# mLSTM cell and hash-routed experts: first step's gate rows moved on the chip, second chunk's gates as a group of their own

## The chip, the cores and the metric

The kernel runs on one core of one Trainium2 chip. The metric is device time in microseconds for one execution; the median of three runs stands for the kernel. Engines are named as the profile names them: PE (TensorE), DVE (VectorE), ACT (ScalarE), POOL (GpSimd), SP (SyncE, which mostly issues DMAs).

## The reference, cut to what matters

Two blocks follow each other. The first is an mLSTM cell over 4 batches, 8 heads, 768 time steps and head dimension 40; the second sends each of the 3072 rows of 320 numbers to one of 8 experts, chosen by a hash of its token id.

```python
for t in range(S):
    m_new = np.maximum(f_gate[:, :, t] + m, i_gate[:, :, t])
    f_stab = np.exp(f_gate[:, :, t] + m - m_new)
    i_stab = np.exp(i_gate[:, :, t] - m_new)
    m = m_new
    C = f_stab[:, :, None, None] * C + i_stab[:, :, None, None] * np.einsum('bhd,bhe->bhde', vt, kt)
    n = f_stab[:, :, None] * n + i_stab[:, :, None] * kt
    h_tilde = np.einsum('bhde,bhe->bhd', C, qt)
    y[:, :, t] = o * h_tilde / denom
...
expert_idx = token_ids * np.int64(2654435761) % np.int64(E)
h = np.maximum(xe @ w1[e], 0.0)
out[mask] = h @ w2[e]
```

## The kernel before, in words

The recurrence is worked out in chunks of 128 time steps. There are 6 chunks and 4 batches, so 24 steps `s`, with batch `b = s % 4` and chunk `c = s // 4`; the loop over them is `for s in range(NT)`. Steps 0 to 3 are the first chunk and need no earlier state. All instructions stand in program order for each engine's queue (`manual_schedule`), so the order written in the code is the order in which an engine takes its work, and an instruction that waits holds up all behind it on that engine. That holds for SP's DMAs too.

A step needs k, q and v of its 128 time steps (`load`, 160 KB each, six buffers of each), and its gates. Inside a chunk, the weight between two time steps is the exponential of a sum of gate terms. The kernel makes that sum by a product of two small bf16 operands: `L`, whose rows 0 to 23 hold the terms of the column's time step (the "ends" e, each split into 3 bf16 pieces, for 8 heads), and `R`, whose rows 32 to 37 hold the terms of the row's time step (A, and from the second chunk on X, 3 pieces each). The other rows of `R` and `L` are constants (selectors, a mask). There are two `L` tiles, one a chunk in turn, and four `R` tiles, one a step in turn.

The class `Gates` computes these terms on DVE for a group of batch-heads and chunks: `sums` gives A, `ends` gives e, `split` makes the 3 pieces (two subtractions), `rows` copies the bf16 halves into the tile `zt` (on ACT), and `weights` makes the factors for k (an exponential on ACT, a transpose on PE, a copy on DVE into `kwT`). There are three groups: `g0` for chunk 0 on 32 partitions, `g1` for chunks 1 to 4 on 128 partitions, `g2` for chunk 5 on 32 partitions, which reuses g0's tiles. `g1` takes its running maxima from `m_d` in DRAM, to which the scan of all 768 time steps (`m_sb`) is written. `keep` writes `zt` to DRAM, `load_a(s)` brings a step's rows back into `R` and `load_e(c)` a chunk's ends into `L`; both are issued by SP. The constant part of `R` is made once in `Rs[0]` and copied on DVE to `Rs[1]`, `Rs[2]`, `Rs[3]`.

A step consists of: `turn` (PE transposes k and q, ACT copies them out of PSUM), `scores` (PE products of k and q, 16 matmuls), `decays` (PE products of `L` and `R` at L333, exponentials on ACT at L337; later chunks also scale q, at L345), `weigh` (DVE multiplies scores by decays, L375), `k_weights` (POOL scales k, L355), `state` (PE, new state, L400), `attend` (PE, L421 and L427) and `divided` (DVE, L436 to L440). In pass `s` of the loop PE takes, in order, `turn(s + 2)`, `scores(s + 1)`, `decays(s + 1)`, `state(s)`, `attend(s)`. The scores' PSUM tiles have one buffer each, so `scores(s + 1)` waits for `weigh(s)`. The tag `tr` (two buffers) serves the transposes, the tag `xh` (two buffers) the results of a step; `divided(s - 1)` frees the buffer that `state(s)` opens.

Before the loop, `unread` makes products that nobody reads (9, 8 and 3 of them). Inside the loop, SP issues in each pass: `load_a(s + 3)`, k and q of step `s + 5`, v of step `s + 4`, then gate loads `o` (listed in `o_at`), and later stores of finished rows. `sigmoid` runs over 8 steps' gates at once at the end of passes 7, 12 and 17. The routing of the experts is cut into pieces that are placed in certain passes (`pieces`, `products`): the transposed ids in pass 4 and a scan of counts in pass 5, for instance. The expert layers come after the loop and are not touched.

## Time and profile before

| | us |
|---|---|
| median of 3 runs | 390.69 |
| lowest and highest run | 388.94, 391.33 |
| profiled execution, its own time | 388.61 |
| its span (first to last instruction) | 386.7 |
| busy in the span: PE, DVE, ACT, POOL | 366.6, 138.0, 113.0, 143.8 |
| mean granted PE clock | 0.987 |

The first stage, the 24 steps, takes about the first 137 us of the span; the expert layers take the rest. In a timeline or chain row the first number is the start in us from the span's start, the second the duration in us, and the arrow in brackets names what ended the engine's idle time before it. `SPq` and `ACTq` rows are DMA issues: the time that the queue's engine took to issue, not the time of the transfer. In the rows of stretches come the stretch and its length, busy us and instruction count of PE, PE's weight loads, DVE, ACT and POOL, then the clock that PE was granted, the mean busy share of the 16 DMA engines, and GB/s.

### The profile page before, as it was taken

To read this page: it belongs to the slowest core of one execution; us is meant where nothing else is said; L and a number is where in the kernel's file an instruction comes from. 1 tells how busy PE (TensorE), PEld (TensorE's weight loads), DVE (VectorE), ACT (ScalarE), POOL (GpSimd) and SP (SyncE) were. 2 spreads that over 40 slices of the span, in tenths; PEclk is the share of its full clock that TensorE was granted. 3 is DMA by queue.
4 is the path that set the end of the run, shared out by engine and by line. 5 is a ranking of instruction groups with operands and counts; after the bars stand their busy time and mean duration, and the time that the engine had idled before them with its cause. 6 is when DMAs were issued, how large, how long until landed. Compare 5 with 4: busy or idle time off the path is not lost.

```text
span 386.7 us, 7979 instructions
## 1 busy us (share of the span) xinstructions
PE 366.6 (95%) x3211; PEld 255.7 (66%) x3211; DVE 138.0 (36%) x355; ACT 113.0 (29%) x232; POOL 143.8 (37%) x247
## 2 busy tenths in 40 slices
PE   7699999899999889999999999999999999999991
PEld 7587788788888666865665655565565665664560
DVE  8657887787878921212012012002102102101100
ACT  5376467576495301111011011111111111101100
POOL 8442555898987317231142140124024020020120
PEclk9789999999999999999999999999999999999998
DMA  6698899989998689382731721442262000000000
GB/s 136 118 175 159 149 171 177 197 191 194 182 232 241 190 272 348 128 251 90 233 108 51 245 97 33 153 160 65 94 215 68 0 34 17 0 35 16 2 26 25
DMA packets 124220, 51.02 MB, mean 132 GB/s; under 512 B 104338, under 2 KB 120174, under 8 KB 124182
## 3 DMA queue, kind: packets, MB, share of 16 engines
q1 hardware_dynamic: 116614, 36.73, 40.7%
q0 software_dynamic: 2496, 8.20, 6.4%
q10 hardware_dynamic: 5072, 5.57, 4.6%
q8 instruction: 26, 0.43, 0.5%
q14 instruction: 12, 0.10, 0.1%
HBM read 42.10 MB, written 8.71 MB: 131 GB/s over the span
## 4 chain that ended last, share of the span: by engine, by line
PE 77%; DVE 8%; issue 6%; POOL 3%; ACT 2%; SPq 2%; DMA 1%; POOLq 0%; DVEq 0%; ACTq 0%
PE mh L858 24%; PE zp L887 23%; PE mh L851 7%; PE sp L369 5%; PE tr L322 5%; PE xh L427 3%; PE ab L333 2%; PE xh L421 2%; PE xh L400 2%; PE tp L834 1%; DVE w L375 1%; PE zp L928 1%; POOL out_dram L821 1%; SPq L193 1%; SPq L189 1%
## 5 line engine op out<-in xcount | busy, mean ns | idle before, releaser
L887 PE MATMUL zp<-w2t,h 128*128 128x320 f32 x384 | 105.5, 433 | 0.0
L858 PE MATMUL mh<-xT,w1t 128*128 128x416 f32 (+2 forms) x288 | 97.0, 481 | 1.3 <-DVE x L440 1.3
L887 PEld LDWEIGHTS zp<-w2t,h 128*128 128x128 f32 x384 | 72.6, 190 | 31.5 <-issue 2.9
L858 PEld LDWEIGHTS mh<-xT,w1t 128*128 128x128 f32 x288 | 51.3, 190 | 39.8 <-issue 37.8
L821 POOL DMA_INDIRECT out_dram<-zo,s_idx x26 | 25.7, 988 | 88.7 <-ACT zo L820 88.4
L840 DVE COPY xT<-tp 128x384 f32<-128x384 f32 x15 | 8.4, 558 | 128.0 <-PE tp L836 128.0
L867 ACT ACTIVATE h<-mh 128x416 f32<-128x416 f32 (+2 forms) x36 | 17.2, 479 | 110.0 <-PE mh L851 59.4
L820 ACT COPY zo<-zp 128x320 f32<-128x320 f32 x26 | 11.1, 426 | 101.3 <-PE zp L887 93.1
L865 DVE TENSOR_SCALAR h<-mh 128x416 f32<-128x416 f32 (+2 forms) x36 | 19.6, 543 | 59.2 <-PE mh L851 31.5
L375 DVE TENSOR_TENSOR w<-sp,w 128x512 f32<-128x512 f32 x48 | 30.8, 682 | 10.7 <-ACT w L337 10.7
L427 PE MATMUL xh<-v,w 128*64 128x41 f32 x768 | 34.6, 222 | 0.0
L337 ACT ACTIVATE w<-ab 128x512 f32<-128x512 f32 x48 | 26.0, 594 | 18.9 <-PE ab L333 18.9
L369 PE MATMUL sp<-qT,kT 64*128 64x128 f32 x384 | 29.5, 291 | 1.7 <-DVE w L375 0.9
L959 POOL COPY hrem<-h 128x256 f32<-128x256 f32 x8 | 3.2, 398 | 74.4 <-ACT h L867 74.4
L427 PEld LDWEIGHTS xh<-v,w 128*64 128x64 f32 x768 | 30.5, 138 | 0.0
L109 POOL DMA_INDIRECT xg<-x_rows,g_idx x24 | 23.4, 973 | 15.6 <-PE mh L851 6.8
L369 PEld LDWEIGHTS sp<-qT,kT 64*128 64x128 f32 x384 | 24.7, 193 | 6.0 <-issue 2.8
L851 PE MATMUL mh<-xT,w1c 64*128 64x416 f32 (+2 forms) x144 | 27.9, 497 | 0.1
L421 PE MATMUL xh<-C,qs 128*64 128x82 f32 x320 | 27.3, 249 | 0.0
L410 POOL TENSOR_TENSOR C<-C,add 64x164 f32<-64x164 f32 x32 | 17.7, 552 | 16.4 <-ACT add L404 15.2
L444 POOL TENSOR_TENSOR x<-x,og 128x320 f32<-128x320 f32 x24 | 20.5, 871 | 6.7 <-DVE x L440 4.9
L355 POOL TENSOR_TENSOR kw<-k,kwT 128x320 f32<-128x320 f32 x20 | 14.4, 723 | 13.1 <-DMA q<-in_q_dram 7.7
(188 smaller groups left out, 388.3 us busy)
## 6 DMA issues: line engine op xcount, KB each, us to landing
w2t<-in_moe_w_dram SPq DMA_DIRECT2D x5, 1280.0 KB
w1t<-in_moe_w_dram SPq DMA_DIRECT2D x5, 1024.0 KB
k<-in_k_dram SPq DMA_DIRECT2D x24, 160.0 KB
v<-in_v_dram SPq DMA_DIRECT2D x24, 160.0 KB
og<-in_o_gate_dram SPq DMA_DIRECT2D x24, 160.0 KB
x_rows<-x SPq DMA_DIRECT2D x24, 160.0 KB
q<-in_q_dram SPq DMA_DIRECT2D x23, 160.0 KB
w2t<-in_moe_w_dram ACTq DMA_DIRECT2D x2, 1280.0 KB
```

The lines of the kernel that those rows point to most:

```text
L109: nc.gpsimd.indirect_dma_start(out=xg, out_offset=None, in_=x_d[:rows, :], in_offset=bass.IndirectOffsetOnAxis(ap=idx, axis=0),)
L337: nc.scalar.activation(w[:, hf], ab[:], AF.Exp)
L369: nc.tensor.matmul(sp[hf][:, j, :], lhsT=d["kT"][r, j, :], rhs=d["qT"][r, j, :], start=True, stop=True)
L375: nc.vector.tensor_tensor(d["w"][:, hf], d["sp"][hf][:], d["w"][:, hf], op=ALU.mult)
L421: nc.tensor.matmul(xh[t, 2 * j : 2 * j + 2, :], lhsT=d["qs"][:, j, t], rhs=Cs[b][c % 2][:, j].rearrange("p h d -> p (h d)"), start=True, s ...
L427: nc.tensor.matmul(hs[t, 2 * j + hf, :], lhsT=d["w"][:, hf, j, t], rhs=d["v"][:, 2 * j + hf, :], start=(c == 0), stop=True, skip_group_che ...
L444: nc.gpsimd.tensor_tensor(x[:], x[:], og[s // NG][:, s % NG], op=ALU.mult)
L821: ins = nc.gpsimd.indirect_dma_start(out=out[:, :], out_offset=bass.IndirectOffsetOnAxis(ap=idx, axis=0), in_=zo[:], in_offset=None, bound ...
L851: nc.tensor.matmul(hp[i][:, : c1 - c0], lhsT=w1c[r, fp, :], rhs=xT[r, 2, c0:c1], start=first, stop=not first,)
L858: nc.tensor.matmul(hp[i][:, : c1 - c0], lhsT=w1t[:, db, fb * P : (fb + 1) * P], rhs=xT[:, db, c0:c1], start=(first and db == 0), stop=(not ...
L865: nc.vector.tensor_relu(h[:, 2 * fp, c0:c1], hp[i][:, : c1 - c0])
L887: nc.tensor.matmul(zp[:], lhsT=h[:, fb, j * P : (j + 1) * P], rhs=w[2][:, fb, :], start=(fb == 0), stop=(fb == FB - 1),)
```

## The change

Chunk 0's rows for step 0 (batch 0) are moved from `zt` straight into `Rs[0]` by six small DMAs (`direct_a`, four on SP and two on ACT), and the ends into `Ls[0]` by one DMA a batch (`direct_e`). A rows for steps 1 to 3 still go through DRAM. k and q of step 2 are issued before the remaining small transfers, v of step 0 after k. The writes of pieces are divided into rows (`keep_a`) and ends (`keep_e`), and the ends are laid out so that `load_e` is one DMA instead of three.

Chunk 1 becomes a group of its own, `ga`, on 32 partitions, with g0's tiles; it takes its maxima from `m_sb` on the chip. `g1` then covers chunks 2 to 4 on 96 partitions; its loads (f1, i1, m1) move into pass 0, its work into passes 1 to 6. `g2`'s work moves to later passes. The copies to `Rs[2]` and `Rs[3]` move behind `weigh(0)` and into pass 0; `load_a(3)` moves into pass 1, `load_a(8)` and `load_e(2)` into pass 6. `unread` is called with 9 and 4. Four of the eight memsets of `Cs` go, and `Ls[1]` and `Lx` are made in pass 0.

```diff
-    z0 = nc.dram_tensor("gate_pieces0", (9, BH, P), BF16, kind="Internal").ap()
-    z1 = nc.dram_tensor("gate_pieces1", (9, (NB - 2) * BH, P), BF16, kind="Internal").ap()
-    z2 = nc.dram_tensor("gate_pieces2", (9, BH, P), BF16, kind="Internal").ap()
+    firsts = (0, 1, 2, NB - 1, NB)
+    zx = [
+        nc.dram_tensor(f"gate_rows{i}", (6, (firsts[i + 1] - firsts[i]) * BH, P), BF16, kind="Internal").ap()
+        for i in range(4)
+    ]
+    ze = [
+        nc.dram_tensor(f"gate_ends{i}", ((firsts[i + 1] - firsts[i]) * BH, 3 * P), BF16, kind="Internal").ap()
+        for i in range(4)
+    ]
...
+        MID = (NB - 3) * BH
+        f1 = gp.tile([MID, P], F32, name="f1")
+        i1 = gp.tile([MID, P], F32, name="i1")
+        m1 = gp.tile([MID, P + 1], F32, name="m1")
...
-        kwT0 = gp.tile([P, BH], F32, name="kwT0")
-        kwT1 = gp.tile([P, P], F32, name="kwT1")
+        kwT = gp.tile([P, (NB - 1) * BH], F32, name="kwT")
...
         def pieces_of(c):
-            return (z0, 0) if c == 0 else (z2, 0) if c == NB - 1 else (z1, (c - 1) * BH)
+            g = max(i for i in range(4) if firsts[i] <= c)
+            return g, (c - firsts[g]) * BH
...
         def load_a(s):
             b, c = place(s)
             n = 3 if c == 0 else 6
-            z, r = pieces_of(c)
-            src = z[:n, r + b * H : r + (b + 1) * H].rearrange("i h t -> i (h t)")
+            g, r = pieces_of(c)
+            src = zx[g][:n, r + b * H : r + (b + 1) * H].rearrange("i h t -> i (h t)")
             nc.sync.dma_start(
                 Rs[s % 4][32 : 32 + n].rearrange("i two h t -> i two (h t)"), src.unsqueeze(1).to_broadcast([n, 2, H * P]),
             )
 
         def load_e(c):
-            z, r = pieces_of(c)
-            for i in range(3):
-                nc.sync.dma_start(
-                    Ls[c % 2][i * H : (i + 1) * H], z[6 + i, r : r + BH].rearrange("(b h) t -> h b t", h=H),
-                )
-
-        def keep(z, zt, rows, eng):
-            eng.dma_start(z[rows].rearrange("i r t -> r i t"), zt[:, rows])
+            g, r = pieces_of(c)
+            nc.sync.dma_start(
+                Ls[c % 2][: 3 * H], ze[g][r : r + BH].rearrange("(b h) (i t) -> (h i) b t", h=H, i=3),
+            )
+
+        def keep_a(g, zt, n, eng):
+            eng.dma_start(zx[g][:n].rearrange("i r t -> r i t"), zt[:, :n])
+
+        def keep_e(g, zt, eng):
+            eng.dma_start(ze[g], zt[:, 6:9].rearrange("r i t -> r (i t)"))
+
+        def direct_a(zt):
+            for j in range(2):
+                for i in range(3):
+                    eng = nc.scalar if i == 2 else nc.sync
+                    eng.dma_start(Rs[0][32 + i : 33 + i, j], zt[:H, i])
+
+        def direct_e(b, zt):
+            nc.sync.dma_start(Ls[0][: 3 * H, b], zt[b * H : (b + 1) * H, 6:9])
 
...
-        load(0, "v")
-        for t, src in ((f1, flat[0]), (i1, flat[1])):
-            nc.sync.dma_start(t[:], src[:, P : S - P].rearrange("r (c t) -> c r t", t=P))
...
-            ind[:], ident[: 3 * H, : 3 * H].rearrange("p (i h) -> p h i", i=3), axis=AX,
+            ind[:], ident[: 3 * H, : 3 * H].rearrange("p (h i) -> p h i", i=3), axis=AX,
...
-            def weights(self, dst):
+            def weights(self, dst, tag="tr"):
                 nc.scalar.activation(
                     self.a[:], self.t["e"][:, 0], AF.Exp, bias=self.t["A"][:, 0, P - 1 : P],
                 )
-                tp = ps.tile([P, self.n], F32, name="tpg", tag="tr", bufs=2)
+                tp = ps.tile([P, self.n], F32, name="tpg", tag=tag, bufs=2)
                 nc.tensor.transpose(tp[:], self.a[:], ident[: self.n, : self.n])
-                nc.vector.tensor_copy(dst[:], tp[:])
+                nc.vector.tensor_copy(dst, tp[:])
...
         g0 = Gates(BH, f0[:], i0[:], m0, "zt0")
-        g1 = Gates(P, f1[:], i1[:], m1, "zt1")
+        second = slice(P, 2 * P)
+        ga = Gates(BH, f_sb[:, second], i_sb[:, second], m_sb[:, P : 2 * P + 1], "zta", g0)
+        g1 = Gates(MID, f1[:], i1[:], m1, "zt1")
         last = slice(S - P, S)
         g2 = Gates(BH, f_sb[:, last], i_sb[:, last], m_sb[:, S - P :], "zt2", g0)
...
-                t, r0 = (kwT0, b * H) if c == 0 else (kwT1, (c - 1) * BH + b * H)
+                r0 = c * BH + b * H
...
         g0.sums(True)
         g0.split("A")
         g0.rows("A", nc.scalar.copy)
-        keep(z0, g0.zt, slice(0, 3), nc.scalar)
+        direct_a(g0.zt)
         g0.ends()
         g0.split("e")
         g0.rows("e", nc.scalar.copy)
-        keep(z0, g0.zt, slice(6, 9), nc.scalar)
+        direct_e(0, g0.zt)
+        keep_a(0, g0.zt, 3, nc.sync)
+        load(2, "k")
+        load(0, "v")
+        direct_e(1, g0.zt)
+        load(2, "q")
         unread(9)
         turn(0, "k")
         turn(0, "q")
         nc.vector.tensor_tensor_scan(m_sb[:, 1:], f_sb[:], i_sb[:], NEG, op0=ALU.add, op1=ALU.max)
+        g0.weights(kwT[:, :BH], "xh")
+        ga.sums(False)
         nc.vector.tensor_copy(Rs[1][:], Rs[0][:])
-        nc.scalar.dma_start(m_d, m_sb[:])
-        load_a(0)
-        load_e(0)
-        nc.vector.tensor_copy(Rs[2][:], Rs[1][:])
-        nc.sync.dma_start(m1[:], bass.AP(tensor=m_d.tensor, offset=m_d.offset + P, ap=[[P, NB - 2], [S + 1, BH], [1, P + 1]]))
-        load_a(1)
-        nc.vector.tensor_copy(Rs[3][:], Rs[2][:])
-        load(2, "k")
-        load(2, "q")
-        load(1, "v")
-        load_a(2)
-        unread(8)
+        turn(1, "k")
+        unread(4)
         scores(0)
-        turn(1, "k")
         turn(1, "q")
         for t in ks[3:] + qs[3:]:
             nc.gpsimd.memset(t[:, :, D:], 0.0)
-        for t in sum(Cs, []):
+        for t in [c[1] for c in Cs]:
             nc.gpsimd.memset(t[:], 0.0)
-        ends_rows(Ls[1])
-        nc.gpsimd.tensor_copy(Lx[:], one[:, 1].to_broadcast([P, HB]))
-        g0.weights(kwT0)
         k_weights(0)
-        for i in range(3, KV - 1):
-            load(i, "k")
-            load(i, "q")
-            load(i - 1, "v")
-        unread(3)
         decays(0)
+        load_a(1)
+        direct_e(2, g0.zt)
+        direct_e(3, g0.zt)
+        nc.scalar.dma_start(m_d, m_sb[:])
+        ga.split("A")
+        ga.ends()
+        load(1, "v")
         weigh(0)
-        g1.sums(False)
-        g1.split("A")
-        g1.ends()
-        g1.split("e")
+        ga.split("e")
+        nc.vector.tensor_copy(Rs[2][:], Rs[1][:])
+        load(3, "k")
+        load(3, "q")
+        load_a(2)
+        load(2, "v")
+        load(4, "k")
+        load(4, "q")
+        load(3, "v")
         nsig, ndone, waiting = -1, 0, {}
...
-            if s + 3 < NT and s not in (1, 2):
+            if s + 3 < NT and s not in (0, 1, 5):
                 load_a(s + 3)
             if s + KV - 1 < NT:
                 load(s + KV - 1, "k")
                 load(s + KV - 1, "q")
             if s == 1:
+                load_a(3)
                 load_a(4)
                 load_e(1)
+            if s == 6:
+                load_a(8)
+                load_e(2)
             if s + KV - 2 < NT:
                 load(s + KV - 2, "v")
-            if b == 0 and 0 < c < NB - 1:
+            if b == 0 and 1 < c < NB - 1:
                 load_e(c + 1)
-            if s == 2:
-                load_a(5)
+            if s == 0:
+                for t, src in ((f1, flat[0]), (i1, flat[1])):
+                    nc.sync.dma_start(t[:], src[:, 2 * P : S - P].rearrange("r (c t) -> c r t", t=P))
+                nc.sync.dma_start(
+                    m1[:], bass.AP(tensor=m_d.tensor, offset=m_d.offset + 2 * P, ap=[[P, NB - 3], [S + 1, BH], [1, P + 1]]),
+                )
             for i in o_at.get(s, ()):
                 load(i, "o")
             if s == 2:
                 nc.sync.dma_start(tok[:], moe_token_ids.rearrange("(b c p) -> c b p", b=B, c=NB))
             if s == 13:
-                keep(z2, g2.zt, slice(0, 9), nc.sync)
+                keep_a(3, g2.zt, 6, nc.sync)
+                keep_e(3, g2.zt, nc.sync)
+            if s == 5:
+                keep_a(2, g1.zt, 6, nc.sync)
+                keep_e(2, g1.zt, nc.sync)
             for i in waiting.pop(s, []):
                 store(i)
...
-            if s == 4:
+            if s == 7:
                 nc.scalar.activation(g2.t["X"][:, 0], g2.t["A"][:, 0], AF.Exp)
-            if s in (5, 8, 11):
-                g2.rows({5: "A", 8: "X", 11: "e"}[s], nc.scalar.copy)
+            if s in (7, 10, 11):
+                g2.rows({7: "A", 10: "X", 11: "e"}[s], nc.scalar.copy)
+            if s in (3, 4):
+                g1.rows({3: "A", 4: "e"}[s], nc.scalar.copy)
+            if s == 2:
+                nc.scalar.activation(g1.t["X"][:, 0], g1.t["A"][:, 0], AF.Exp)
...
             if s == 0:
-                nc.scalar.activation(g1.t["X"][:, 0], g1.t["A"][:, 0], AF.Exp)
-                g1.rows("A", nc.scalar.copy)
+                nc.scalar.activation(ga.t["X"][:, 0], ga.t["A"][:, 0], AF.Exp)
+                ga.rows("A", nc.scalar.copy)
...
             if s == 0:
-                g1.split("X")
-                g1.rows("e", nc.scalar.copy)
-                g1.rows("X", nc.scalar.copy)
-                keep(z1, g1.zt, slice(0, 9), nc.sync)
+                ga.split("X")
+                ga.rows("e", nc.scalar.copy)
+                ga.rows("X", nc.scalar.copy)
+                keep_a(1, ga.zt, 6, nc.sync)
+                keep_e(1, ga.zt, nc.sync)
+                nc.vector.tensor_copy(Rs[3][:], Rs[2][:])
+                ends_rows(Ls[1])
+                nc.gpsimd.tensor_copy(Lx[:], one[:, 1].to_broadcast([P, HB]))
...
+            if s == 1:
+                g1.sums(False)
             if s == 2:
-                g1.weights(kwT1)
+                ga.weights(kwT[:, BH : 2 * BH])
+                g1.split("A")
+                g1.ends()
             if s == 3:
+                g1.split("e")
+                g1.split("X")
+                g1.rows("X", nc.scalar.copy)
+            if s == 5:
                 g2.sums(False)
-            if s == 4:
+            if s == 6:
+                g1.weights(kwT[:, 2 * BH :])
                 g2.split("A")
-            if s == 6:
+            if s == 9:
                 g2.split("X")
             if s == 10:
                 g2.ends()
```

More of the change, by code (lines that the diff above doesn't have):

```diff
@@ L166 @@
         m_sb = gp.tile([BH, S + 1], F32, name="m_sb")
-        f1 = gp.tile([P, P], F32, name="f1")
-        i1 = gp.tile([P, P], F32, name="i1")
-        m1 = gp.tile([P, P + 1], F32, name="m1")
+        MID = (NB - 3) * BH
+        f1 = gp.tile([MID, P], F32, name="f1")
+        i1 = gp.tile([MID, P], F32, name="i1")
+        m1 = gp.tile([MID, P + 1], F32, name="m1")
         ones = gp.tile([P, P], F32, name="ones")
         tok = gp.tile([NT, P], I64, name="tok")
-        kwT0 = gp.tile([P, BH], F32, name="kwT0")
-        kwT1 = gp.tile([P, P], F32, name="kwT1")
+        kwT = gp.tile([P, (NB - 1) * BH], F32, name="kwT")
         st, og = {}, {}
@@ L353, in k_weights @@
                 d["kw"] = kws[s % 2]
-                t, r0 = (kwT0, b * H) if c == 0 else (kwT1, (c - 1) * BH + b * H)
+                r0 = c * BH + b * H
                 nc.gpsimd.tensor_tensor(
                     d["kw"][:, :, :D], d["k"][:, :, :D],
-                    t[:, r0 : r0 + H].unsqueeze(2).to_broadcast([P, H, D]), op=ALU.mult,
+                    kwT[:, r0 : r0 + H].unsqueeze(2).to_broadcast([P, H, D]), op=ALU.mult,
                 )
```

## The prediction

> **What bounds the kernel now.** I read the page first: PE is busy 95% of the span, so what counts is where PE is held up or slowed. Next the stretches of 5 us at the start, the only place where the granted clock falls (us busy and count per engine, clock, DMA share, GB/s):
>
> ```profile
> 10.00:15.00 5.00, 2.80 (x21) 1.89 (x19) 3.08 (x5) 2.44 (x5) 3.84 (x5) 0.95 0.25 51
> 15.00:20.00 5.00, 4.21 (x26) 3.31 (x28) 3.29 (x11) 1.17 (x2) 0.00 (x0) 0.50 1.14 202
> 20.00:25.00 5.00, 5.00 (x80) 4.12 (x82) 2.71 (x8) 4.16 (x10) 1.77 (x7) 0.87 1.00 181
> 25.00:30.00 5.00, 5.00 (x112) 4.43 (x108) 2.49 (x7) 3.52 (x8) 2.51 (x13) 1.00 0.76 143
> ```
>
> From 10 to 15 us PE has 2.80 us of work and the DMA engines stand three quarters idle; then the clock is at half: 0.05, 0.50 and 0.13 of a full clock lost in three rows of 5 us, so from about 14.5 to 21.3, 6.8 us. Why, the chain of what ended last in order of time tells (start, us, what):
>
> ```profile
> 6.74 1.74 DVE m_sb L685
> 8.48 1.98 DVE R L686
> 10.48 0.99 DVE R L690
> 11.49 0.99 DVE R L693
> 13.06 2.51 DMA k<-in_k_dram
> ```
>
> The loads of step 2 are issued at 13.06, behind gate-row transfers that wait for DVE and for a write to DRAM. The waits agree, SP's first, then PE's (us in total, times, longest):
>
> ```profile
> SPq L203 <- DMA gate_pieces<-zt: 3.2, 2, 2.3
> PE tr L322 <- DMA k<-in_k_dram: 1.7, 1, 1.7
> ```
>
> ACT's timeline dates the steps, the exponentials of decays(0) to decays(4):
>
> ```profile
> 13.79 1.08 ACT L337 ACTIVATE w<-ab 128x512 f32<-128x512 f32 x2 [1.76 <-PE ab L333]
> 20.59 1.09 ACT L337 ACTIVATE w<-ab 128x512 f32<-128x512 f32 x2 [2.00 <-PE ab L333]
> 25.05 1.09 ACT L337 ACTIVATE w<-ab 128x512 f32<-128x512 f32 x2 [0.24 <-PE ab L333]
> 29.10 1.09 ACT L337 ACTIVATE w<-ab 128x512 f32<-128x512 f32 x2 [0.80 <-PE ab L333]
> 33.97 1.08 ACT L337 ACTIVATE w<-ab 128x512 f32<-128x512 f32 x2 [0.85 <-PE ab L333]
> ```
>
> The full pace is 4.05 us (25.05 to 29.10); decays(0) to decays(1) takes 6.80. So some 4 us could be won before decays(3). SP's queue is the other resource, here with what it issues for decays(2), (3) and the second chunk:
>
> ```profile
> 14.83 0.58 SPq L203 DMA_DIRECT2D R<-gate_pieces  x1
> ...
> 20.86 0.46 SPq L203 DMA_DIRECT2D R<-gate_pieces  x1
> ...
> 23.73 0.37 SPq L215 DMA_DIRECT2D gate_pieces<-zt  x1
> ...
> 27.15 0.29 SPq L203 DMA_DIRECT2D R<-gate_pieces  x1
> ```
>
> Between the first two stand seven loads of 160 KB: 6.03 us, 0.86 a load. R of decays(3) is issued at 20.86, 7.8 us before PE uses it at 28.65.
>
> **The change, part by part.** Times are from the span's start, by durations of these rows.
>
> Rows of step 0 on the chip. Two ACT issues of 0.36 follow the A copy (ends 6.21), so the e copy starts at 6.95 instead of 6.84: 0.1, not on PE's path. SP issues four row DMAs, the ends DMA and the write of the A rows (0.29 to 0.46 each in its rows for R and L), then k2 and v0: k2 goes out near 8.4 (before 13.06) and lands near 10.9 by the chain's 2.51. How soon an on-chip transfer lands no row shows; bounded by R's (10.47 to the products at 13.35, 2.9) and by no gain over its 0.3 of issue, it lies between 8 and 10.6 for issues up to 7.7. Cover: PE gets to decays(0) only near 12.6, so either end costs nothing.
>
> PE's order up to decays(0). ACT copies kT0 and qT0 until 8.6 and makes the weights' exponential (0.40) by 9.05; PE then does tpg 0.24, k1's transposes 0.6, four dummy products 0.94, scores 1.16, q1's transposes 0.6, and the ab products of decays(0) start at 12.6. ACT's copy of q1 (0.59) goes first: exponentials at 13.2 against 13.79, 0.6 won. DVE has copied kwT at 9.6, does ga's sums (1.0) and R1's copy (0.98) until 11.7, ga's A split and ends (1.2) until 12.9, and weighs from 13.8 to 15.1: what was added is hidden in DVE's wait, which was 1.85 here.
>
> Step 1. k2 and q2 are in; scores(1) waits for the weighing and ends at 16.2; R1 was issued at 11.75 and is in. decays(1)'s exponentials come at 16.6: 4.0 ahead. Step 2 follows at the old pace, 20.8 against 25.05.
>
> SP from there is what decides. load_a(2) waits for R2's copy on DVE: weighing ends 15.1, ga's e split 0.6, copy 0.98, so 16.7. SP stands until then, and v2, k4, q4, v3, k5, q5, v4 are queued behind it. Then come the new f1, i1 (0.73, 0.54), m1 (0.55), two writes of ga's pieces (0.37 each), k6 and q6, and only then load_a(3). Lower bound, each at its quickest issue (k 0.4, q 0.57, v 0.4, with 0.05 between): 7.3 us, issue at 24.0. Upper bound, 0.86 for each of nine loads and 3.0 for the rest: 10.7 us, 27.4. I take 25.9, about the middle: the DMA engines start empty near 17 (q3 out at 14.3, and 2.51), but are then given loads faster than they move them. Landing: 2.51 (k2's) to 2.84 us later (the chain has a row `53.28 2.84 DMA R<-gate_pieces`), so R3 is in at 28.4 (26.5 to 30.2). PE has been ready since scores(3), at 24.4. The exponentials of decays(3) follow its first product by 0.45 (28.65 to 29.10), so they come at 28.85 instead of 29.10: of the 4.0 us won, 0.25 is left (1.9 down to -1.5). The wait stands in PE's order before state(2) and attend(2), so nothing else fills it.
> DVE has a second wait here: g1's sums of step 1 need f1, i1 and m1, in near 26; behind them divided(1) (1.1) ends at 28.0, which state(2) waits for. It lies beside R3's wait and costs nothing unless R3 comes before 28.
>
> The clock after that wait. PE stands 4.0 us (24.4 to 28.4). In the trace the clock fell at 14.5 with PE at work for 2.80 us of the five before, its longest wait by then 1.0 us. So I expect another half-clock stretch. Ends: 0, and 3.4 us lost (6.8 at half). I take half of it, 1.7, as PE is dense afterwards, where at 15 to 18 it still waited.
> The Trainium skill (TensorE: Matmul & The Clock Gate, Part 1) has the clock fall after at least one idle window of about 3.4 us and rise after one busy window. By it a 4.0 us wait may or may not fill a free-running window, and would cost 0 or 1.7; here the clock fell without any such wait, so I keep the rows' reading.
>
> Later steps. decays(4) finds R4 and L1 in: the second chunk's pieces are written near 24 instead of 23.73. Step 4 loses g2's A split on DVE (0.27 + 0.48), which held up the copy that q6's successor on PE waited for by 0.24: -0.24 (0 to -0.75). Step 5 gets g2's sums (0.71 + 0.28 + 0.41) ahead of the routing scan, where DVE had 0.39 idle: 0 to 1.1, taken 0.4, since state(7) waited for divided(6) there. Step 6 gets g1's weights: one more transpose, 0.33 (0.24 to 0.8: the row's own time, and with the 0.47 that PE waited for it in step 2). Step 7 needs R8 and L2, whose loads now stand behind k11 and q11: SP was through with those near 51.0, so by 2.84 they would land at 53.9 and 54.3, and decays(8) began at 54.06. SP has three L loads less to issue before that (2.35 us from 40.42) and two writes more: 0 (0 to 1.5). Step 8 loses the X copy between sigmoid and exponentials, 0.4 on the chain. Steps 2 and 3 get 1.2 us of g1's splits on DVE in place of g2's sums (1.4) and of DVE's idle time before qs: 0. The copies of A and e (0.51 each on ACT) lie in ACT's waits for transposes, 1.3 to 1.75 a step; if those go, 0.5 each.
> Fewer L loads (one DMA for three, five times) save SP about 0.7 a time, off the path. POOL writes Ls[1] and Lx (2.5 us) in step 0 instead of before kw: it had 7.7 idle there, and without that kw(2) would start up to 2.5 later.
>
> Sum: -0.25 + 1.7 - 0.24 + 0.4 + 0.33 - 0.4 = +1.54. On the profiled execution (388.61, span 386.7 and 1.9 around it) that is 390.15; the median of the runs, 390.69, lies 2.08 above it, so 392.2. About 1% (3.9 us) is what a measurement of this kernel can tell from no change.
>
> **The rivals.**
> The clock holds through the wait for R3: the same sum without 1.7, so 390.5. For: PE runs at 1.00 in every stretch from 25 to 140 us. Against: the fall at 14.5 us.
> R3 comes in time. If SP gets load_a(3) out by 22, f1 to m1 land by 23.5, divided(1) ends at 25.6 and state(2) starts there instead of at 29.10: -3.5, with the later terms' +0.09 on top 387.3. For: SP's rows hold issues of 0.3 to 0.4 us. Against: 6.03 us for seven loads, and here there are nine and five small ones.
> A cold start, on the slower side. Dummy products fall from 20 to 13, and PE waits from 6.4 to 9.1. If the clock halves at about 11.0, 2.1 us of PE work is left before decays(0)'s exponentials (scores 1.05, q1 0.6, half of ab 0.4) and takes twice as long; the weighing ends at 17.2, load_a(2) goes out at 18.8 and R3 is in at 30.5: +2.1 on the sum, 394.3. It decides from where decays(0)'s exponentials start after 15. For: 2.80 us of PE work in five was already enough for a fall. Against: from 9.1 on PE has no gap over 1 us.
> The same page (Part 4: PE-mode transpose) says that transposes do not count as PE-busy in the same way for the gate. That speaks for this rival, as PE's early work is mostly transposes; no row here separates the two.
>
> **How the numbers follow.** The main sum 0.46, clock holds 0.20, R3 in time 0.15, cold start 0.19. Predicted is the main one, 392.2. The range goes down to 387.0 (R3 in time, with a little over half of it inside) and up to 395.2 (the cold start with 0.9 us of the unknown costs), leaving out about 0.2. Faster by over 1% (below 386.8) is the half of R3 in time in which the later terms take their lower ends too (step 4 -0.75, step 5 0): 0.08. Slower by over 1% (above 394.6): 0.4 of the cold start and the upper end of the main case (clock 3.4, step 5 1.1, step 6 0.8, step 7 1.5), 0.20. Within 1%: 0.72.
>
> **What would show it.** Right: exponentials at about 13, 16.6, 20.8, then 28.9; PE idle for some 4 us before line L333 in step 2, released by a DMA of the gate rows; load_a(3) issued after 25; a half-clock stretch near 28 to 32. Wrong: exponentials every 4.05 us from 16.6 on; first exponentials after 15; or a total that moves by over 4 us.

## The result, and the profile after

The changed kernel takes 395.78 us (median of 4 runs, 395.50 to 396.26) against 390.84 (4 runs) for the kernel before: a ratio of 1.0142, 95% interval 1.0111 to 1.0172. It is slower, by 3.6 us more than predicted, and 0.6 us above the range. The profiled execution took 395.50 us with a span of 393.6 (before: 388.61 and 386.7).

In the changed kernel the lines have moved: exponentials L354, products of `L` and `R` L350, transposes L339, row loads L210, on-chip rows L230, on-chip ends L233, `divided` L453 to L457. First ACT's timeline, which dates the steps 0 to 5, with what stands before the first:

```profile
6.23 1.97 ACTq L230 DMA_DIRECT2D R<-zt  x2
8.24 0.51 ACT L312 COPY zt<-e_zt 32x384 bf16<-32x384 bf16 x1 [2.04 <-DMA R<-zt]
...
16.70 0.60 ACT L354 ACTIVATE w<-ab 128x512 f32<-128x512 f32 x1
...
20.21 1.08 ACT L354 ACTIVATE w<-ab 128x512 f32<-128x512 f32 x2 [1.45 <-PE ab L350]
...
24.30 1.11 ACT L354 ACTIVATE w<-ab 128x512 f32<-128x512 f32 x2
...
33.53 1.09 ACT L354 ACTIVATE w<-ab 128x512 f32<-128x512 f32 x2 [0.93 <-PE ab L350]
...
39.27 1.08 ACT L354 ACTIVATE w<-ab 128x512 f32<-128x512 f32 x2 [0.40 <-PE ab L350]
...
45.09 1.08 ACT L354 ACTIVATE w<-ab 128x512 f32<-128x512 f32 x2
```

The first exponentials are 3.5 us later than predicted (16.70 for 13.2), the fourth 4.7 (33.53 for 28.85). PE's timeline has the two waits that go with these:

```profile
10.06 0.31 PE L324 MATMUL tpg<-ident,a_zt 32*128 32x32 f32 x1 [3.30 <-ACT a_zt L320]
...
32.86 1.06 PE L350 MATMUL ab<-R,L 128*64 128x512 bf16 x4 [4.62 <-DMA R<-gate_rows]
```

SP's timeline shows the queue behind the second of them: the on-chip rows, k of step 2, `load_a(2)`, then f1, i1, m1, the second chunk's pieces, and last `load_a(3)`:

```profile
6.23 2.89 SPq L230 DMA_DIRECT2D R<-zt  x4
...
10.49 0.43 SPq L199 DMA_DIRECT2D k<-in_k_dram  x1
...
19.76 0.26 SPq L210 DMA_DIRECT2D R<-gate_rows  x1
...
25.30 0.81 SPq L759 DMA_DIRECT2D f<-in_f_gate_dram  x1
...
26.94 0.69 SPq L760 DMA_DIRECT2D m<-gate_max  x1
27.74 0.39 SPq L221 DMA_DIRECT2D gate_rows<-zt  x1
...
29.94 1.70 SPq L210 DMA_DIRECT2D R<-gate_rows  x2
```

Stretches of 3.4 us, laid so that the changes of the granted clock fall on their borders (columns as before: PE's busy time is the first after the length, the clock the third from the end):

```profile
6.10:9.50 3.40, 0.67 (x6) 0.42 (x4) 2.30 (x4) 1.36 (x4) 2.56 (x15) 1.00 0.02 3
9.50:12.90 3.40, 2.84 (x13) 2.71 (x13) 2.42 (x5) 1.09 (x3) 2.21 (x3) 0.51 0.48 83
12.90:16.30 3.40, 3.40 (x24) 2.68 (x24) 1.82 (x5) 0.08 (x1) 1.56 (x3) 0.50 0.53 93
...
26.60:30.00 3.40, 1.64 (x22) 1.28 (x19) 0.00 (x0) 1.07 (x2) 1.31 (x9) 1.00 0.53 109
30.00:33.40 3.40, 0.54 (x4) 0.21 (x4) 1.91 (x7) 0.31 (x1) 0.00 (x0) 0.50 0.70 131
33.40:36.80 3.40, 3.40 (x54) 3.16 (x51) 1.37 (x3) 2.07 (x5) 0.00 (x0) 0.50 1.00 179
```

So the clock is at half twice, for 6.8 us each: from 9.5, after a window in which PE worked for 0.67 us, and from 30.0, in the middle of the wait for R3. Both the predicted wait and the rival "cold start" have come.

Where the 6.9 us of the two profiled executions lie is read from the starts of the exponentials (columns other than the first two kernels belong to the experiments below):

| step | before | after | a4 | c1 | e2 | b1 | b2 | d2 |
|---|---|---|---|---|---|---|---|---|
| 0 | 13.79 | 16.70 | 15.47 | 15.54 | 13.99 | 13.69 | 13.67 | 14.47 |
| 1 | 20.59 | 20.21 | 18.98 | 19.05 | 17.52 | 17.19 | 17.17 | 17.97 |
| 3 | 29.10 | 33.53 | 28.52 | 27.87 | 26.65 | 26.28 | 25.92 | 26.72 |
| 5 | 38.23 | 45.09 | 40.29 | 40.10 | 36.38 | 35.41 | 35.05 | 35.85 |
| 7 | 49.69 | 55.20 | 51.31 | 51.12 | 47.26 | 47.52 | 47.23 | 48.04 |
| 8 | 54.52 | 60.59 | 58.00 | 56.51 | 54.30 | 52.34 | 52.06 | 52.87 |
| 9 | 61.49 | 67.85 | 65.50 | 63.75 | 63.42 | 61.27 | 59.04 | 59.85 |
| 11 | 69.82 | 76.18 | 73.83 | 72.08 | 71.76 | 72.26 | 67.37 | 68.19 |

Differences of the first two columns: +4.43 us at step 3, +2.43 from step 3 to 5, -1.35 from 5 to 7, +0.56 from 7 to 8, +0.29 from 8 to 9: 6.36, which then stays (6.36 at step 11).

An exponential can also be late by ACT's own doing, so PE's products of `L` and `R`, which it follows, are the better mark for PE. At steps 3, 5, 7, 8 and 9 they start at 28.65, 37.78, 49.24, 54.07 and 58.90 before and at 32.86, 43.17, 54.76, 60.15 and 64.98 after: +4.21 us at step 3, +1.18 from 3 to 5, +0.13 from 5 to 7, +0.56 from 7 to 8, nothing from 8 to 9. The loss lies at step 3.

### The profile page after: what moved, and what is told of

Same layout as the page of the kernel before. It is cut to its first block, busy times and chain, and to the rows that moved or that the text cites. A ratio compares the mean times of both kernels' runs of the same rounds, so it can differ in the third digit from the quotient of the medians.

```text
span 393.6 us, 7972 instructions
## 1 busy us (share of the span) xinstructions
PE 368.3 (94%) x3198; PEld 257.6 (65%) x3198; DVE 142.0 (36%) x367; ACT 114.1 (29%) x237; POOL 143.2 (36%) x243
## 4 chain that ended last, share of the span: by engine, by line
PE 79%; DVE 8%; issue 5%; POOL 3%; ACT 2%; DMA 1%; ACTq 0%; SPq 0%; POOLq 0%; another core or an unknown queue 0%; DVEq 0%
PE mh L904 23%; PE zp L933 23%; PE mh L897 7%; PE sp L386 5%; PE tr L339 5%; PE xh L444 4%; PE ab L350 3%; PE xh L438 2%; PE xh L417 2%; DVE w L392 2%; PE tp L880 1%; PE zp L974 1%; POOL out_dram L867 1%; PE xb L358 1%; DVE qs L362 1%
## 5 line engine op out<-in xcount | busy, mean ns | idle before, releaser
L444 PE MATMUL xh<-v,w 128*64 128x41 f32 x768 | 35.5, 225 | 0.0
L444 PEld LDWEIGHTS xh<-v,w 128*64 128x64 f32 x768 | 31.5, 141 | 0.0
L354 ACT ACTIVATE w<-ab 128x512 f32<-128x512 f32 x48 | 26.1, 595 | 15.3 <-PE ab L350 15.3
L438 PE MATMUL xh<-C,qs 128*64 128x82 f32 x320 | 27.4, 249 | 0.0
```

What stands on the lines that cost most here:

```text
L354: nc.scalar.activation(w[:, hf], ab[:], AF.Exp)
L438: nc.tensor.matmul(xh[t, 2 * j : 2 * j + 2, :], lhsT=d["qs"][:, j, t], rhs=Cs[b][c % 2][:, j].rearrange("p h d -> p (h d)"), start=True, s ...
L444: nc.tensor.matmul(hs[t, 2 * j + hf, :], lhsT=d["w"][:, hf, j, t], rhs=d["v"][:, 2 * j + hf, :], start=(c == 0), stop=True, skip_group_che ...
```

## The experiments

Theories at the start. A: R3's late load holds step 3. B: the cold start delays all of it. C: g1's sums, which wait on DVE for m1, would hold step 3 as long as R3 does. D: the separate group for the second chunk costs in steps 3 to 9. Each ratio is to the kernel before, on the same chip.

### a1: R3 loaded earlier

```diff
         nc.vector.tensor_copy(Rs[2][:], Rs[1][:])
+        nc.vector.tensor_copy(Rs[3][:], Rs[2][:])
...
             if s == 0:
+                load_a(3)
                 for t, src in ((f1, flat[0]), (i1, flat[1])):
...
             if s == 1:
-                load_a(3)
                 load_a(4)
...
-                nc.vector.tensor_copy(Rs[3][:], Rs[2][:])
```

> The changed kernel with one thing undone in SP's order: the copy to Rs[3] stands beside that to Rs[2], and load_a(3) goes out in pass 0 before f1, i1 and m1, as before the change. Theory A (SP's queue: R3 is late because load_a(3) stands behind gate loads, piece writes, k6 and q6): PE's 4.62 us wait for R3 and the half clock behind it go, 5 to 6 us faster than the changed kernel, about 390. Theory C (DVE: g1's sums wait 4.95 us for m1 on DVE, and divided(1) behind them holds state(2)): the wait only moves from the ab products to state(2), which starts near 33 instead of 33.9, at most 1 us faster, about 395. Theory B (the cold start decides everything) expects no more than 1 us either.

396.15 us, ratio 1.0161 [1.0109, 1.0214]: nothing gained. R3 is in, and PE's products for step 3 run at 27.55. But the exponentials start at 32.31, because DVE stands before g1's sums (DVE's timeline of a1), with `divided(1)` behind them, and ACT stands with it before the exponential of `X`, which needs the sums:

```profile
31.00 0.29 DVE L299 TENSOR_TENSOR a_zt<-f,m 96x128 f32<-96x128 f32 x1 [5.92 <-DMA m<-gate_max]
```

A alone falls; C holds.

### a2: a1, and g1's sums one pass later

```diff
-            if s == 1:
-                g1.sums(False)
             if s == 2:
                 ga.weights(kwT[:, BH : 2 * BH])
+                g1.sums(False)
```

(The exponential of `X` moves with it, to pass 3.)

> As the last one, and g1's sums move from pass 1 to the end of pass 2 (its X exponential to pass 3). Theory A with C: both waits that end near 33 are gone, decays(3) at about 28.5 and every step after it 4 to 5 us earlier, no half clock at 30: 5 to 6 us faster than the changed kernel, 390 to 391. If A alone were right it would equal the last run within 0.5. If B alone were right, both stay near 395.

394.08 us, ratio 1.0111 [1.0053, 1.0169]. Step 3 starts at 28.60, 4.9 us earlier than in the changed kernel; at step 5 only 2.25 of that are left (42.84), since PE now waits 2.02 us for the second chunk's ends at step 4 and the clock falls at 35.4. A and C together are real, but pay less than expected.

### a3: PE kept busy at the start

```diff
         turn(0, "q")
+        unread(8)
         nc.vector.tensor_tensor_scan(m_sb[:, 1:], f_sb[:], i_sb[:], NEG, op0=ALU.add, op1=ALU.max)
```

> The changed kernel with eight of the dummy products put back, where PE waits for ACT (6.76 to 10.06). Theory B (the half clock from 9.5 to 16.4 delays the weighing of step 0, with it the copy to Rs[2], load_a(2) and all of SP's queue): no half clock at the start, first exponentials at about 14.3 instead of 16.7, load_a(2) at 17.4 instead of 19.76, R3 in near 30.4, 2 to 2.5 us faster, about 393.5. Theory A alone (SP's rate of issue sets R3, whenever it starts): under 1 us. PE's wait for R3 stays at 4 us or more in both.

393.79 us, ratio 1.0105 [1.0052, 1.0157]: the clock holds at the start and the first exponentials come at 13.99, 2.7 us earlier than in the changed kernel. But step 3 is only 1.25 us earlier (32.28), and the clock still falls during R3's wait, at 29.2. SP's timeline of a3 shows the two row loads:

```profile
17.29 0.40 SPq L210 DMA_DIRECT2D R<-gate_rows  x1
...
28.64 1.73 SPq L210 DMA_DIRECT2D R<-gate_rows  x2
```

`load_a(2)` goes out 2.47 us earlier than in the changed kernel, `load_a(3)` 1.30. B holds, at 2.0 us by the times and 1.4 by the ratios, where 2 to 2.5 was expected. The eight products do not always keep the clock up: a4, c1, c2 and e1 have them too, and in their profiled executions it falls at 11.2 to 11.6, with the first exponentials near 15.5.

### a4: a2 and a3 together

> The three edits together. If the waits of A and C and the cold start of B add up, 5 to 6 and 2 to 2.5: 387.5 to 389, faster than before the change by 2 to 3 us. If R3, m1 and the clock are one chain, whose first cause is the cold start, no better than 390.

392.69 us (10 runs), ratio 1.0086 [1.0063, 1.0108], slower than either forecast: 2 us of the loss are gone, 3.4 are not. Step 3 is now ahead of the kernel before (28.52 against 29.10); steps 3 to 5 take 11.77 us against 9.13, and 7 to 8 take 6.69 against 4.83. This is D.

### c1: a4, with the third group's pieces earlier

```diff
         for s in range(NT):
             b, c = place(s)
+            if s == 5:
+                keep_a(2, g1.zt, 6, nc.sync)
+                keep_e(2, g1.zt, nc.sync)
+            if s == 6:
+                load_a(8)
+                load_e(2)
             if s + 3 < NT and s not in (0, 1, 5):
                 load_a(s + 3)
```

(The same lines are taken from their old places behind the loads.)

> The three edits together (392.7), and in SP's queue the writes of g1's pieces go out at the head of pass 5 and the loads of R8 and L2 at the head of pass 6, ahead of that pass's other DMAs. Theory: step 7 to step 8 takes 6.69 us there (4.83 before the change) because PE waits for L2 and R8; with them earlier it takes 4.9, so 1.8 us faster than the three edits, 390.9. If that wait only hides the one for the o loads at the sigmoid, under 0.5.

391.28 us, ratio 1.0067 [1.0048, 1.0086]. Step 7 to 8 takes 5.39 instead of 6.69: the wait was SP's order, as expected.

### c2: c1, with g1's splits and ends behind `divided`

```diff
             if s == 2:
                 g1.sums(False)
-                g1.split("A")
-                g1.ends()
-            if s == 3:
-                g1.split("e")
-                g1.split("X")
...
+            if s == 3:
+                g1.split("A")
+                g1.ends()
+            if s == 4:
+                g1.split("X")
+                g1.split("e")
```

(The additions stand behind `divided(s - 1)` and ahead of `scores(s + 1)`; `rows` follows them.)

> As the last one, and g1's splits and ends go on DVE behind divided and ahead of the scores of passes 3 and 4, where DVE waited for PE's xb products, instead of at the ends of passes 2 and 3. Theory (the new group's DVE work stands in the chain weights, splits, divided, qs, weigh): steps 3 to 5 take 9.1 to 9.5 us as before the change instead of 11.8; 2.3 to 2.6 us faster than the last one, 388.4. Rival (DVE is full in these passes, so the work costs the same anywhere): within 0.7 of the last one.

391.34 us, ratio 1.0082 [1.0056, 1.0108]: no gain, but because two things cancel. PE's wait at step 4 for the second chunk's ends, which SP loads behind everything that pass 0 issues, stays as it was in c1 (1.60 us there; c2's PE timeline):

```profile
33.94 0.62 PE L350 MATMUL ab<-R,L 128*64 128x512 bf16 x4 [1.69 <-DMA L<-gate_ends]
```

From PE's products of step 5 to those of step 6 c2 takes 5.00 us instead of 6.70, so the splits' new place is worth 1.7. But from step 4 to 5 it takes 5.79 instead of 4.27, since the clock is at half from 35.4 to 38.8, which it is not in c1. The mean clocks of the four runs (0.984 to 0.990, c1 0.992 to 0.996) say that it was lower in all of them.

### d1: the early rows and loads, with the old grouping

One group for chunks 1 to 4 as before, `firsts = (0, 1, NB - 1, NB)`; rows on the chip, k and q of step 2 early, eight dummy products, R1 to R3 copied in a row.

> One part of the change alone: rows of step 0 moved on the chip and step 2's loads ahead, with the old grouping (g1 for chunks 1 to 4 on 128 partitions, its work where it was) and load_e as one DMA; eight dummy products stand where PE waits for ACT, and Rs[1] to Rs[3] are copied one after the other, so that no load waits for a weighing. Theory (the direct rows and early loads are worth some 3 us by step 3, and the group of its own is what costs): exponentials of step 3 at 26 to 27.5 instead of 29.10, later steps as before the change: 386.5 to 388, 2 to 3.5 us faster than before. Rival (the direct DMAs themselves cost more than they save, 1.9 us of issue on ACT before the weights): step 3 at 28.5 or later, 389 to 391.

393.36 us, ratio 1.0129 [1.0092, 1.0165], for a reason of its own: g1's sums, ahead of `weigh(1)` on DVE, waited for an m1 that this order loads late (waits of d1):

```profile
DVE a_zt L299 <- DMA m<-gate_max: 3.7, 1, 3.7
```

Steps 3 to 5, however, take 9.13 us (31.13 to 40.26), exactly as before: the extra time there belongs to the separate group.

### b1: only the third step's loads, in the kernel before

```diff
         nc.scalar.dma_start(m_d, m_sb[:])
+        load(2, "k")
+        load(2, "q")
         load_a(0)
...
-        load(2, "k")
-        load(2, "q")
         load(1, "v")
```

> The kernel before, with k and q of step 2 issued ahead of SP's wait for the write of the first gate rows, and nothing else. Theory (PE's wait of 1.74 us for k2 and the half clock from 14.5 to 21.3 come from that order alone): step 0 at most 0.5 later (its rows are issued behind two loads), step 1 at 18.0 to 18.8 instead of 20.59, later steps as before: 1.5 to 2.5 us faster than before, about 388. Rival (R of steps 1 to 3 and v0 to v2 slip by the same): no change within 0.5.

389.29 us (10 runs), ratio 0.9999 [0.9967, 1.0031]. Steps 1 to 8 are 2.2 to 3.4 us earlier, and at step 9 all but 0.22 is gone, since the sigmoid on ACT waits for gate loads that SP issues only 1.0 us earlier than before (50.76 for 51.77; b1's ACT timeline):

```profile
55.93 1.28 ACT L361 ACT_TABLE_LOAD   x1 [1.97 <-DMA og<-in_o_gate_dram]
...
61.27 1.08 ACT L337 ACTIVATE w<-ab 128x512 f32<-128x512 f32 x2
```

PE then stands idle and the clock falls (at 61.8): in the profiled execution step 11 starts 2.4 us later than in the kernel before.

### b2: b1, and the first eight gate loads one pass earlier

```diff
-        for i, j in enumerate((3, 3, 4, 4, 5, 5, 6, 6, 7, 8,
+        for i, j in enumerate((2, 2, 3, 3, 4, 4, 5, 5, 7, 8,
```

> The kernel before with k2 and q2 issued ahead of load_a(0), as in b1, and the first eight o loads one pass earlier (passes 2 to 5 instead of 3 to 6). If b1 lost its 2.2 to 3.4 us at step 9 only because the sigmoid waited for the last o load (in at 55.9), the o loads now are in near 51, step 9 starts near 59 (61.3 in b1) and the clock does not fall there: 387.0 against 389.3 on this pair, ratio 0.994. If SP and the DMA engines are simply full up to there, the o loads push k, q and v back instead, a later step waits for those, and the time stays at that of the kernel before, ratio 0.999 to 1.001.

387.02 us (12 runs) against 389.39 (23 runs), ratio 0.9943 [0.9920, 0.9967]: faster than both kernels. The sigmoid no longer waits, step 9 is 2.45 us ahead of the kernel before, and the clock holds through the 24 steps:

```profile
53.69 1.28 ACT L361 ACT_TABLE_LOAD   x1
...
59.04 1.08 ACT L337 ACTIVATE w<-ab 128x512 f32<-128x512 f32 x2
```

### d2: b2 and the first step's rows on the chip

```diff
-        keep(z0, g0.zt, slice(0, 3), nc.scalar)
+        direct_a(g0.zt)
...
-        keep(z0, g0.zt, slice(6, 9), nc.scalar)
+        direct_e(0, g0.zt)
+        keep_a(0, g0.zt, 3, nc.sync)
+        load(2, "k")
+        load(2, "q")
+        direct_e(1, g0.zt)
...
-        load_a(0)
-        load_e(0)
```

> b2 and the first step's rows moved on the chip, with the old grouping of the gates (128 partitions) and the old order of everything else: the first and second parts of the change without the third. If the third part (a group of its own for the second chunk) is what costs, this is not slower than b2: within 0.5 us of it, 386.5 to 387.5, and steps 3 to 5 take 9.1 us as in the kernel before. If the row transfers themselves cost (0.6 to 0.7 us of issue each on SP, two of 0.6 to 1.3 on ACT), the loads behind them are late: 389 to 391.

388.10 us (12 runs), ratio 0.9960 [0.9937, 0.9983]. Steps 3 to 5 take 9.13 us: the first two parts without the third do no harm against the kernel before. But every step up to 12 is 0.8 us later than in b2, and the median is 1.1 us above b2's (the intervals overlap; the two profiled executions meet again at step 19 and have the same span, 385.3). In d2, ACT's timeline has the same first lines as the changed kernel's (1.97 us of issues, the ends copied at 8.24); in b2 it reads:

```profile
6.23 0.36 ACTq L215 DMA_DIRECT2D gate_pieces<-zt  x1
6.83 0.51 ACT L297 COPY zt<-e_zt 32x384 bf16<-32x384 bf16 x1 [0.63 <-DVE e_zt L293]
...
13.67 1.08 ACT L337 ACTIVATE w<-ab 128x512 f32<-128x512 f32 x2 [1.65 <-PE ab L333]
```

### e1 and e2: c1 and c2, with the second chunk's pieces first

```diff
                 keep_a(1, ga.zt, 6, nc.sync)
                 keep_e(1, ga.zt, nc.sync)
...
+                for t, src in ((f1, flat[0]), (i1, flat[1])):
+                    nc.sync.dma_start(t[:], src[:, 2 * P : S - P].rearrange("r (c t) -> c r t", t=P))
...
+                load_a(4)
+                load_e(1)
+                load(5, "k")
+                load(5, "q")
+                load(4, "v")
```

(These and m1's load stood ahead of `keep_a(1)` or, the loads of step 4's rows and ends, in pass 1.)

> c1 with the writes and loads of the second chunk's pieces issued ahead of k5, q5 and v4, and f1, i1, m1 between them. If steps 3 to 5 lose their 2.5 us because the pieces are late in SP's queue (PE's wait for load_a(4) and load_e(1) there), R and L of step 4 are in near 30 instead of 33.8, steps 3 to 5 take near 10.0 us instead of 12.2: 389.3 against 391.3 for c1 (ratio 1.002). If the loss is DVE's work for the separate group (splits ahead of divided), nothing is gained: 391.

e1: 394.00 us (4 runs), ratio 1.0102 [1.0041, 1.0162], a miss. R and L of step 4 are issued by 26.95 and PE no longer waits for them, but k5, now behind them, holds PE for 0.95 us, and the clock falls twice, at 11.2 and at 31.7.

> e1 with the third group's splits and ends on DVE behind divided of passes 3 and 4, as in c2. If pieces and splits both held steps 3 to 5, they now take 9.2 us and the time is 388.5; if only the pieces did, it is that of e1, 389.3; if neither, 391.

e2: 394.54 us (4 runs, 390.91 to 397.38), ratio 1.0155 [1.0095, 1.0215], a miss as a time. The profiled execution is the quickest of the four, and in it the clock never falls before the expert layers: steps 3 to 5 take 9.73 us and steps 3 to 7 20.61 (20.59 before the change), so pieces and splits did hold them together. Step 7 is 2.43 us ahead of the kernel before. But the steps now run into later loads. At step 8 it is the third group's ends, issued only 0.7 us earlier than in e1 (50.50 for 51.18; e2's waits), and at the sigmoid ahead of step 9 the gate loads, as in b1 (e2's ACT timeline):

```profile
PE ab L350 <- DMA L<-gate_ends: 1.6, 1, 1.6
```

```profile
58.48 1.28 ACT L378 ACT_TABLE_LOAD   x1 [2.57 <-DMA og<-in_o_gate_dram]
```

Step 9 comes at 63.42, 1.93 us behind the kernel before. What the other three executions lost is not profiled; a mean clock of 0.985 against 0.994 in the one that took 396.39 us says that the clock was lower there.

### f1 and f2: all six on-chip rows issued by SP

```diff
-                    eng = nc.scalar if i == 2 else nc.sync
-                    eng.dma_start(Rs[0][32 + i : 33 + i, j], zt[:H, i])
+                    nc.sync.dma_start(Rs[0][32 + i : 33 + i, j], zt[:H, i])
```

> The changed kernel with all six on-chip row transfers issued by SP, none by ACT. If ACT's two issues (1.97 us) cause the cold start, ACT's ends copy starts near 6.85 instead of 8.24, the transposes of the weights near 8.7 instead of 10.06, the clock does not fall at 9.5, and the first exponentials come at 14 to 15 instead of 16.70; SP's k2 goes out 1.3 us later (11.8, in at 14.3), so step 1 is at 17.8 to 18.6 instead of 20.21. R3's wait stays (step 3 at 32 to 33), so the time is that of a3, ratio 1.010. If PE's early idle has another cause, the clock falls as before and the time is that of the changed kernel or 1 us more, ratio 1.014 to 1.017.

f1 is the changed kernel with this edit: 395.88 us, ratio 1.0176 [1.0145, 1.0207]. ACT's timeline:

```profile
6.84 0.51 ACT L311 COPY zt<-e_zt 32x384 bf16<-32x384 bf16 x1 [0.63 <-DVE e_zt L307]
...
13.93 0.60 ACT L353 ACTIVATE w<-ab 128x512 f32<-128x512 f32 x1
...
19.51 0.60 ACT L353 ACTIVATE w<-ab 128x512 f32<-128x512 f32 x1 [1.19 <-PE ab L349]
```

The first exponentials come 2.77 us earlier. Of this, 1.40 is the transpose of the weights (8.66 for 10.06): ACT's issues delayed it, as the theory has it. The rest is the clock, at half for 3.4 us there instead of 6.8. But it still falls without ACT's issues, at 8.3, PE having waited 2.28 us, so they alone do not make the cold start. The total does not follow, against the expectation: SP's two extra issues make k2 and q2 late (k2 out at 11.86), PE waits 1.79 us for q2 and the clock falls again at 18.5, step 1 comes at 19.51, and step 3, at 33.50, where it was.

> d2 with all six on-chip row transfers issued by SP. If ACT's issues are what makes d2 0.8 us later than b2, the first exponentials come at 13.5 to 13.9 instead of 14.47 and the time is that of b2, ratio 0.994 to the kernel before (d2 0.996). If it is how long the rows take to arrive, the first exponentials stay at 14.4 or later, now with 1.3 us more of issues ahead of the ends rows on SP: ratio 0.996 to 0.999.

f2 is d2 with the edit: 389.81 us (12 runs), ratio 1.0010 [0.9990, 1.0030], worse than d2. The first exponentials are at 13.65, so ACT's issues were d2's 0.8 us; but SP now issues rows for 4.12 us and k2 goes out at 12.44 (SP's timeline):

```profile
6.96 4.12 SPq L229 DMA_DIRECT2D R<-zt  x6
...
12.44 0.43 SPq L199 DMA_DIRECT2D k<-in_k_dram  x1
```

PE waits for it (1.49 us), the clock falls at 17.0, step 1 comes at 18.83. The price of the rows is their issue, on whichever queue it lies.

## Why the prediction was right or wrong

The direction was right, and the main mechanism too: `load_a(3)` at the end of SP's queue, PE idle before L350, a second fall of the clock. The sum was +1.54 us; at step 9, past all that the change touches early, it came out at +6.36.

**`load_a(3)` (the step that failed).** "SP from there is what decides" was right, but the prediction took 25.9 for the issue, with 24.0 and 27.4 as bounds, and it came at 29.94. R3 landed 2.78 us after its issue, as priced, at 32.72. So "-0.25" at step 3 became +4.43: 4.68 of the 4.82 us that the sum was short at step 9. The other terms missed by less, and nearly cancel. a2 is the test: with R3's late load and the equal wait on DVE taken away, step 3 is 4.9 us earlier.

The issue came late by 4.04 us for two reasons. The queue starts late, since `load_a(2)` goes out at 19.76 instead of 16.7; and from there it takes 10.18 us where 9.2 was taken. The second weighs more than these numbers say: where the queue starts early it takes longer, 11.35 us in a3 (from 17.29) and 11.94 in f1 (17.97 to 29.91), both above the upper bound of 10.7. With `load_a(2)` within 0.6 us of its forecast, a3 still has `load_a(3)` at 28.64. The bound was too low: the rows between R of steps 2 and 3 in the kernel before hold six loads, not seven (15.46 to 20.86), so 0.90 us a load instead of 0.86, and the five small transfers take 3.5 us in the changed kernel where 2.6 and 3.0 were counted. What sets SP's pace there no run shows.

**ACT's two issues and the cold start.** These are why the queue starts late. The prediction gave "two ACT issues of 0.36" and the ends copy at 6.95. They took 1.97 and the copy started at 8.24. The 0.36 was that of a write to DRAM; for a transfer from partitions to one partition on the chip there was no row, and neither bound nor range was set for its issue, only for its landing. The transpose of the weights comes at 10.06 for 9.05, 1.0 late. From it to the products of decays(0) PE then takes 6.05 us (10.06 to 16.11) where 3.55 was taken, as the clock is at half: 2.5 more. With it the first exponentials go from 13.2 to 16.70. PE's wait in front was in the prediction ("PE waits from 6.4 to 9.1"), but only under a rival; f1 shows that the clock can fall after it without ACT's issues too.

**SP's row DMAs.** "0.29 to 0.46 each" were 0.72 in the mean (2.89 for four, 0.72 for the ends): k2 out at 10.49 instead of 8.4. In the changed kernel the late start covers this, in f2 it decides.

**The second wait on DVE.** "Costs nothing unless R3 comes before 28" was right as it stands, but g1's sums could start only at 31.19, when m1 was in, not near 26, so that this wait was as long as R3's (a1): undoing the forecast wait alone was worth nothing.

**The clock after the wait.** 1.7 was taken; half clock lasts until 36.8 and PE works from 32.86 on, so (36.8 - 32.86) / 2 = 2.0, which is near.

**Steps 3 to 5.** With the clock's 1.7 and step 4's -0.24 the prediction has +1.46 there. The exponentials give +2.43, PE's products +1.18. The difference is ACT at step 5: g1's copy of `X`, which waits for DVE's splits, stands ahead of the copy of kT there (the chain of waits, then PE's products of step 5):

```profile
43.08 0.09 DVE den L453
43.18 0.51 ACT zt L312
43.69 0.02 issue
43.71 0.59 ACT kT L340
```

```profile
43.17 0.62 PE L350 MATMUL ab<-R,L 128*64 128x512 bf16 x4
```

So the exponentials come 1.92 us after their products, where it was 0.45 before. By step 7 the exponentials have caught up, and that is the -1.35 from 5 to 7: 1.47 of lag gone, 0.13 added on PE. PE itself waits only 0.56 us for the copy of kT. So "Steps 2 and 3 get 1.2 us of g1's splits on DVE ... : 0" is wrong by at most that in the changed kernel. It is wrong by more once R3's wait is gone: from step 3 to 7 a4 takes 22.79 us against 20.59, c1 23.25, and only e2, which moves the pieces and the splits, is back at 20.61.

**Later steps.** Of the +0.73 for steps 5 to 7 PE's products show +0.13. The 0.4 for g2's sums came to nothing: step 6 to 7 takes 5.85 us on PE in both kernels. The 0.33 for g1's weights lies between steps 7 and 8, where +0.56 was measured: their transpose (0.30 us, at 57.82), and `state(6)`, which starts 0.51 us instead of 0.22 after the products ahead of it. c1 has the same, so it is not R8 and L2: "Step 7 needs R8 and L2: 0 (0 to 1.5)" was right here. Step 8's -0.4 was +0.29 at the exponentials: the copy of `X` is gone, but ACT now waits 0.83 us for DVE just ahead of the sigmoid.

**The rivals.** "A cold start" came with its own test, first exponentials after 15. It was priced as +2.1 on the main sum, 394.3 in all, which is 1.5 us under the 395.78 measured: the fall was put at 11.0 and came at 9.5, so that more of PE's work was at half speed, and SP's longer queue is missing from it. "R3 in time" is what a4 to e2 try to make, and its forecast of 387.3 is not reached by any of them: 391.28 is the best, because in each a late load, a split or a fall of the clock is left in the way.

**What was left open.** What sets the pace of SP's queue, and what e2's three unprofiled executions lost, was not settled. A separate group without on-chip rows was not tried.

## What to carry to other kernels

Where an early stage runs ahead of its loads, ask first which later load it will run into: b1's 2 to 3 us were lost at step 9 and kept by moving eight loads (b2), and a load moved to the end of an in-order queue waits for all that stands ahead of it (10.18 us here). Small transfers are paid by the engine that issues them, so count every issue on each queue, and price a kind of transfer that no row shows from well below and well above. When two waits end together, taking away one is worth nothing; look for the second before the first is undone.

## What the runs showed of the hardware

**The clock goes by a fixed grid of 3.4 us, and a long wait isn't needed.** In the 16 profiled executions all changes of the granted clock of one execution lie multiples of 3.41 us apart. Counting PE's busy time in the windows of that grid, the 20 falls before the end all came after windows with 0.00 to 1.92 us of PE work; of the windows that were not followed by a fall five had less than 1.92 (1.60, 1.68, 1.81, 1.83 and 1.86). The fall that the kernel before shows at 14.5, with no wait over 1.01 us after PE's first work, is of this kind (its stretches):

```profile
11.10:14.50 3.40, 1.73 (x11) 1.05 (x11) 1.51 (x4) 1.64 (x5) 2.80 (x4) 1.00 0.19 44
14.50:17.90 3.40, 2.11 (x9) 1.44 (x9) 3.20 (x9) 0.96 (x2) 0.00 (x0) 0.50 1.16 206
```

The Trainium skill (TensorE: Matmul & The Clock Gate, Part 1) describes a free-running window of 3413 ns, and the grid agrees with it. It speaks of "≥1 idle window" before a fall; here windows a little more than half filled with work (1.71 to 1.92 us of 3.41) were enough. The same place says that the moment of the change varies from run to run with the window's phase. The runs agree: e1 and e2 have the same code up to the second step, and differ in where the grid lies. First e1, then e2:

```profile
7.80:11.20 3.40, 1.13 (x10) 1.09 (x11) 1.49 (x4) 2.03 (x5) 1.45 (x4) 1.00 0.07 12
11.20:14.60 3.40, 3.40 (x24) 2.95 (x23) 3.30 (x7) 0.32 (x1) 3.20 (x5) 0.50 0.84 148
```

```profile
8.90:12.30 3.40, 2.23 (x23) 2.07 (x25) 1.88 (x5) 1.71 (x4) 1.67 (x3) 1.00 0.26 45
12.30:15.70 3.40, 3.04 (x29) 1.96 (x26) 3.33 (x8) 2.11 (x5) 2.10 (x3) 1.00 0.82 148
```

The same gap, cut by a border at 11.2 in one and at 8.9 and 12.3 in the other, costs the first 1.5 us at the first exponentials (15.53 against 13.99). So a gap of 1 to 2 us that is harmless in one execution need not be in the next.

**Small transfers on the chip are slow to issue.** One row of 8 heads from eight partitions to one: 0.62 to 0.84 us on SP, and 1.27 and 0.66 on ACT (1.97 for the two), where a row load from DRAM took 0.26 to 0.58 at that stage and a write 0.36.
